# A fused attention and gated-MLP block: strided q, k, v weights, a new opening and one ring of weight tiles

## The chip, the cores and the metric

The kernel runs on one core of a Trainium2 chip. The metric is the device time of one execution in microseconds; lower is better. A core has a matrix engine (TensorE, PE in the rows; its weight loads are shown apart as PEld), VectorE (DVE), ScalarE (ACT), GpSimd (POOL) and SyncE (SP, which here only issues DMA transfers). The engines run at the same time, each through its own list of instructions in order, and wait for each other by semaphores. Matrices come from DRAM into on-chip memory (SBUF, 128 partitions); TensorE writes its results into PSUM, from where VectorE or ScalarE takes them out.

## The reference

One sequence of 2048 rows and 1024 columns, all in bf16:

```python
xn = layernorm(x)                                  # x: 2048 x 1024
q, k, v = split(xn @ wqkv)                         # 32 heads of 32 columns each
# a row attends to itself and to rows s-2, s-4, ... s-14 (W = 8, dilation 2), rows below 0 masked
attn = softmax(mask(q . k[s - 2w]) * 32 ** -0.5)   # over the 8 offsets w
s = (sum over w of attn * v[s - 2w]) @ wo
g = silu((silu(xn @ w1) * (xn @ w3)) @ w2)         # inner width 3584
out = x + s * g
```

## The kernel before

The rows are worked in four chunks (c) of 512. Within a chunk everything is held transposed: xnT has the 1024 columns of xn on partitions, as 8 tiles (kt) of 128, and 512 rows of the chunk along the free side. A group is eight matmuls that add up over kt into one PSUM tile of 128 x 512, each with its own weight tile of 128 x 128 as the stationary side.

TensorE's work in a chunk, in order: 24 groups for q, k, v (qkv, L291; 192 matmuls); 14 gate/up blocks (up_block, L261; four groups each, 448 matmuls) that give 28 tiles h; the first half of the down projection (down_half, L449; 112 matmuls); of the second half three steps of 16 matmuls; the output projection of attention (wo_proj, L420; 64 matmuls); and the other four steps. In the last chunk the output projection comes before the second half (last_half, L487). Chunk 0 is opened by hand (L503 to L668): layernorm of four row tiles, their transposes on TensorE, then two gate/up blocks (LEAD), of which the first one's groups are computed in halves of 256 rows (part0, L591), then its q, k, v groups, then the other 12 blocks.

Attention is done by VectorE beside TensorE. The columns of q, k, v are dealt so that a partition holds one head and one of four quarters (r) of its columns, and 8 columns (j) lie along the free side. Products of q with shifted k are summed over j into E; 16 GpSimd transfers (shuffle_out, L341) bring E into the layout L4 with heads and row quarters on partitions; softmax is done there; 16 more transfers (shuffle_back, L382) bring the weights pb back into Pr; products with shifted v are joined into oT, which the output projection reads.

The dealing needs every eighth weight column in one stationary tile. Before, the q, k, v weights were loaded as they are (raw), copied by VectorE and ScalarE into the dealt order (permute, L516; 24 copies of 128 x 1024) in chunk 0, used from there (pm), and written to a DRAM scratch wperm, from which chunks 1 to 3 load tiles of 256 columns. The heads' order on partitions is r, then head.

Order: the program's order is fixed by hand. Work for VectorE, ScalarE and GpSimd that lies beside TensorE is put into a list (Side, L17) with an estimated cost; after each group, side.step adds the group's time (GRP, 1.727) to a clock and a credit, and takes items off the list while there is credit and an item's due time has come. side.flush takes out what is left; wo_proj begins with it.

Queues: SP issues the weight tiles (512 KB each) in the order of use, each as soon as its buffer is free. There are two rings: wstream with 6 tiles for q, k, v, w1, w3 (load_w, L150) and w2s with 3 for w2 (load_w2, L175). In the last three gate/up blocks of a chunk load_w is not called (AHEAD); late_w calls it in the down projection. The weights of the output projection (load_wo, L189; 8 transfers of 256 KB) are issued after block 10, the residual rows xres after step 4 of the first down half. GpSimd issues the shuffles and most of the output.

Of the kernel before, what the change touches and what calls it, by code (L numbers as in the profile page):

```python
# [45 lines left out]
def kernel(  # L46
# [11 lines left out]
    nc = tc.nc  # L58
# [11 lines left out]
    NR = 4  # L70
    GRP = 1.727
    LEAD = 2
    WO_AT = 3
    AHEAD = 3
# [7 lines left out]
    wo_r = A_wo.rearrange("(h r j) n -> r h j n", r=NR, j=NJ)  # L82
# [3 lines left out]
    dram = ctx.enter_context(tc.tile_pool(name="dram", bufs=1, space=bass.MemoryType.DRAM))  # L86
# [5 lines left out]
    wstream = ctx.enter_context(tc.tile_pool(name="wstream", bufs=6))  # L92
    w2s = ctx.enter_context(tc.tile_pool(name="w2s", bufs=3))
# [9 lines left out]
    wperm = dram.tile([KT, P, 3 * NJ, P], BF16, name="wperm")  # L103
# [4 lines left out]

    x0 = [xp.tile([P, D], BF16, tag="x", name=f"x0_{st}") for st in range(NST)]
    for st in range(NST):  # L110
        nc.sync.dma_start(out=x0[st][:], in_=x_flat[st * P:(st + 1) * P, :])
    eps_t = const.tile([P, 1], FP32, name="eps_t")
# [23 lines left out]

    w_list = []
    for fb in range(LEAD):
        w_list += [("1", fb), ("3", fb)]
    for fb in range(LEAD, FB):  # L140
        w_list += [("1", fb), ("3", fb)]
    for c in range(1, NCH):
        w_list += [("q", b) for b in range(12)]
        for fb in range(FB):
            w_list += [("1", fb), ("3", fb)]
    w_list += [("2", fb) for fb in range(4)]
    w_next = iter(w_list)
    w_tiles = deque()

    def load_w():  # L150
        item = next(w_next, None)
        if item is None:
            return
        kind, i = item
        wt = wstream.tile([P, KT, 2 * P], BF16, tag="w")
        if kind == "q":
            src, dst = wperm[:, :, 2 * i:2 * i + 2, :].rearrange("kt kp tj p -> kp kt (tj p)"), wt[:]
        elif kind == "2":
            src = w2_r[:, i * 4:(i + 1) * 4, 512:1024]
            dst = wt[:].rearrange("p a b -> p (a b)").rearrange("p (i n) -> p i n", n=512)  # L160
        else:
            src, dst = (w1_r if kind == "1" else w3_r)[:, :, i * 256:(i + 1) * 256], wt[:]
        nc.sync.dma_start(out=dst, in_=src)
        w_tiles.append((item, wt if kind != "2" else dst))

    def take_w(item):
        got, wt = w_tiles.popleft()
        assert got == item, (got, item)
        return wt

    w2_list = [(c, dh, fb) for c in range(NCH) for dh in range(2) for fb in range(7) if (c, dh) != (NCH - 1, 1) or fb >= 4]
    w2_next = iter(w2_list)
    w2_tiles = deque()

    def load_w2():  # L175
        item = next(w2_next, None)
        if item is None:
            return
        c, dh, fb = item
        wt = w2s.tile([P, 4, 512], BF16, tag="w2")  # L180
        nc.sync.dma_start(out=wt[:], in_=w2_r[:, fb * 4:(fb + 1) * 4, dh * 512:(dh + 1) * 512])
        w2_tiles.append((item, wt))

    def take_w2(item):
        got, wt = w2_tiles.popleft()
        assert got == item, (got, item)
        return wt

    def load_wo():  # L189
        was = []  # L190
        for dh in range(2):
            wa = block("wo").rearrange("p (j n) -> p j n", n=CH)
            for r in range(NR):
                nc.sync.dma_start(out=wa[r * 32:(r + 1) * 32, :, :], in_=wo_r[r, :, :, dh * 512:(dh + 1) * 512])
            was.append(wa)
        return was
# [11 lines left out]

# [38 lines left out]

    brings = deque()

    def bring_one():  # L250
        if brings and brings[0][0] <= side.now:
            brings.popleft()[1]()

# [7 lines left out]
    def up_block(c, xnT, fb):  # L261
        hts = []
        w1t, w3t = take_w(("1", fb)), take_w(("3", fb))
        for i in range(2):
            pss = []
            for wt in (w1t, w3t):
                ps = psum_mm.tile([P, CH], FP32, tag="mm", name=f"gu{c}_{fb}_{len(pss)}")
                for kt in range(KT):
                    nc.tensor.matmul(  # L269
                        ps[:], lhsT=wt[:, kt, i * P:(i + 1) * P], rhs=xnT[:, kt, :],  # L270
                        start=(kt == 0), stop=(kt == KT - 1),
                    )
                pss.append(ps)
            if i == 1 and fb < FB - AHEAD:
                load_w()
                load_w()
# [5 lines left out]

    def proj_group(ps, lhs, xnT):
        for kt in range(KT):
            nc.tensor.matmul(ps[:], lhsT=lhs(kt), rhs=xnT[:, kt, :], start=(kt == 0), stop=(kt == KT - 1))  # L285

# [4 lines left out]
    def qkv(c, xnT):  # L291
        nc.gpsimd.tensor_copy(out=kT[:, :, 0:HALO], in_=kT[:, :, CH:CH + HALO])
        nc.gpsimd.tensor_copy(out=vT[:, :, 0:HALO], in_=vT[:, :, CH:CH + HALO])
        for b in range(12):
            wt = take_w(("q", b))
            for i in range(2):
                t, j = divmod(2 * b + i, NJ)
                ps = psum_mm.tile([P, CH], FP32, tag="mm", name="ps_qkv")
                proj_group(ps, lambda kt: wt[:, kt, i * P:(i + 1) * P], xnT)
                if i == 1:  # L300
                    load_w()
# [442 lines left out]
```

## Time and profile before

| what | value |
|---|---|
| median of 3 runs | 825.02 us (822.5 to 826.67) |
| profiled execution, span | 824.7 us |
| TensorE busy | 813.0 us, 99% |
| VectorE, ScalarE, GpSimd busy | 479.7, 206.8, 92.3 us |
| DMA, mean | 185 GB/s, 152.69 MB |

No time is given for the profiled execution beside its span; the span lies inside the three times. Times in the rows are microseconds from the span's start, and a row of a group gives busy time and mean ns of one instruction. In a row of the timeline stand start, length, engine, line, operation, output<-input, partitions x elements and, in brackets, how long the engine had been idle and what released it. A matmul's length in the rows includes its way through the pipeline, so the pace is read from the starts of neighbouring runs.

### The profile page before, as it was taken

What the parts mean: (1) busy time and instruction counts of PE and PEld (TensorE: products, weight loads), DVE (VectorE), ACT (ScalarE), POOL (GpSimd) and SP (SyncE); (2) the same over time, 40 slices, a digit from 0 to 9 for tenths busy, and PEclk for the clock granted to TensorE, in tenths of its full rate; (3) what the DMA queues carried; (4) which work ended last, traced back from release to release, by engine and by line L of the source; (5) the groups of instructions that cost most, each with busy time, mean ns of one, the idle gap of its engine ahead of it and who ended that gap; (6) DMA issues with size and microseconds to landing.
All of it is one profiled execution on the core that took longest, in us unless ns stands there. A gap on an engine that the chain in (4) does not pass through costs nothing.

```text
span 824.7 us, 9542 instructions
## 1 busy us (share of the span) xinstructions
PE 813.0 (99%) x3823; PEld 373.1 (45%) x3823; DVE 479.7 (58%) x486; ACT 206.8 (25%) x319; POOL 92.3 (11%) x172
## 2 busy tenths in 40 slices
PE   8999999998999999999999999999999999999998
PEld 5444444443444444444444444444444444444444
DVE  5739775594209947494222977569312595649432
ACT  6742132012232133101233213310113321311120
POOL 0000213101100041200110021300011004030010
PEclk9999999999999999999999999999999999999999
DMA  9992889692455698939355489995925557684820
GB/s 296 354 344 60 223 195 207 164 314 88 154 153 146 193 211 193 238 106 312 107 179 153 132 223 195 209 186 159 300 81 179 151 152 185 176 205 98 260 98 26
DMA packets 221821, 152.69 MB, mean 185 GB/s; under 512 B 19536, under 2 KB 208592, under 8 KB 221776
## 3 DMA queue, kind: packets, MB, share of 16 engines
q1 hardware_dynamic: 216336, 140.00, 62.3%
q0 software_dynamic: 5440, 12.07, 6.4%
q8 instruction: 30, 0.49, 0.3%
q14 instruction: 15, 0.12, 0.1%
HBM read 130.02 MB, written 10.49 MB: 170 GB/s over the span
## 4 chain that ended last, share of the span: by engine, by line
PE 90%; DVE 4%; DMA 3%; issue 1%; ACT 1%; POOL 0%; SPq 0%; DVEq 0%; ACTq 0%
PE gu L269 38%; PE ps_qkv L285 20%; PE acc L459 20%; PE ps_wo L428 7%; PE acc L495 3%; DMA Pr<-pb 2%; PE gu L285 1%; DVE pv L397 1%; DMA wt<-wperm 1%; DVE ht L258 1%; PE gu L594 1%; DVE stats L200 1%; DMA x<-in_A_x_dram 0%; POOL Pr L386 0%; ACT L256 0%
## 5 line engine op out<-in xcount | busy, mean ns | idle before, releaser
L269 PE MATMUL gu<-xnT_next,wt 128*128 128x512 bf16 x1344 | 290.6, 379 | 0.0
L269 PEld LDWEIGHTS <-wt 128*128 128x128 bf16 x1728 | 169.1, 98 | 203.9
L459 PE MATMUL acc<-wt,ht 128*128 128x512 bf16 x784 | 170.5, 379 | 0.8 <-DVE ht L258 0.8
L258 DVE TENSOR_TENSOR ht<-sg,gu 128x512 bf16<-128x512 bf16 x112 | 75.8, 680 | 95.6 <-PE gu L269 70.5
L256 ACT ACTIVATE sg<-gu 128x512 bf16<-128x512 f32 x112 | 65.9, 597 | 255.8 <-PE gu L269 230.3
L285 PE MATMUL ps_qkv<-xnT_next,wt 128*128 128x512 bf16 x576 | 124.8, 379 | 0.0
L315 DVE TENSOR_TENSOR prod<-qT,kT 128x4096 bf16<-128x4096 bf16 x32 | 73.1, 2285 | 85.8 <-ACT kT L289 85.8
L459 PEld LDWEIGHTS <-ht 128*128 128x128 bf16 x784 | 76.7, 98 | 93.5 <-issue 1.1
L285 PEld LDWEIGHTS <-wt 128*128 128x128 bf16 x608 | 59.5, 98 | 71.5
L445 DVE TENSOR_TENSOR gt<-gt,s_sb 128x512 f32<-128x512 f32 (+1 forms) x33 | 22.2, 673 | 119.4 <-ACT gt L439 73.0
L269 PE MATMUL gu<-xnT,wt 128*128 128x512 bf16 x384 | 83.0, 379 | 0.0
L345 POOL DMA_DIRECT2D L<-E x64 | 37.1, 587 | 292.5 <-DVE E L330 191.2
L397 DVE TENSOR_TENSOR pv<-Pr,vT 128x4096 bf16<-128x4096 bf16 x28 | 63.2, 2284 | 0.0
L326 DVE TENSOR_TENSOR prod<-prod 128x2048 bf16<-128x2048 bf16 x64 | 61.1, 955 | 1.4
L428 PE MATMUL ps_wo<-wo,oT 128*128 128x512 bf16 x256 | 57.6, 387 | 3.5 <-DMA wt<-wperm 3.5
L439 ACT ACTIVATE gt<-acc 128x512 f32<-128x512 f32 (+1 forms) x33 | 19.3, 584 | 147.6 <-PE acc L459 126.1
L386 POOL DMA_DIRECT2D Pr<-pb x64 | 36.8, 583 | 110.9 <-DVE pb L379 100.5
L447 POOL DMA_DIRECT2D out_dram<-o_t x28 | 15.3, 547 | 296.2 <-DVE o_t L446 295.0
L285 PE MATMUL ps_qkv<-xnT,pm 128*128 128x512 bf16 x192 | 41.9, 379 | 1.1 <-DVE pm L519 1.1
L428 PEld LDWEIGHTS <-oT 128*128 128x128 bf16 x256 | 25.4, 100 | 35.2 <-DVE oT L408 4.0
L432 ACT CAST s_sb<-ps_wo 128x512 bf16<-128x512 f32 x32 | 18.7, 585 | 72.9 <-PE ps_wo L428 72.9
L408 DVE TENSOR_TENSOR oT<-oT,pv 128x4096 bf16<-128x4096 bf16 x16 | 36.6, 2288 | 0.3
(69 smaller groups left out, 364.2 us busy)
## 6 DMA issues: line engine op xcount, KB each, us to landing
wt<-in_B_w_dram SPq DMA_DIRECT2D x168, 512.0 KB, 4.7
wt<-wperm SPq DMA_DIRECT2D x36, 512.0 KB, 4.9
wo<-in_A_wo_dram SPq DMA_DIRECT2D x32, 256.0 KB, 9.4
raw<-in_A_wqkv_dram SPq DMA_DIRECT2D x6, 1024.0 KB, 9.8
wperm<-pm SPq DMA_DIRECT2D x6, 1024.0 KB, 11.6
L<-E POOLq DMA_DIRECT2D x64, 64.0 KB, 5.9
Pr<-pb POOLq DMA_DIRECT2D x64, 64.0 KB, 5.6
xres<-in_A_x_dram SPq DMA_DIRECT2D x4, 1024.0 KB, 7.3
```

Of the source, the lines that this page charges most:

```text
L256: nc.scalar.activation(out=sg[:], in_=g_ps[:], func=ACTF.Silu)
L258: nc.vector.tensor_mul(ht[:], sg[:], u_ps[:])
L269: nc.tensor.matmul(ps[:], lhsT=wt[:, kt, i * P:(i + 1) * P], rhs=xnT[:, kt, :], start=(kt == 0), stop=(kt == KT - 1),)
L285: nc.tensor.matmul(ps[:], lhsT=lhs(kt), rhs=xnT[:, kt, :], start=(kt == 0), stop=(kt == KT - 1))
L315: nc.vector.tensor_mul(prod, qT[:], kT[:, :, o:o + CH])
L326: nc.vector.tensor_add(prod[:, 0:n, :], prod[:, 0:n, :], prod[:, n:2 * n, :])
L345: nc.gpsimd.dma_start(out=L4[sq * 32:(sq + 1) * 32, r, :, :], in_=E[r * 32:(r + 1) * 32, :, sq * P:(sq + 1) * P],)
L386: nc.gpsimd.dma_start(out=Pr[r * 32:(r + 1) * 32, :, sq * P:(sq + 1) * P], in_=pb[sq * 32:(sq + 1) * 32, :, :],)
L397: nc.vector.tensor_mul(dst, Pr[:, w, :].unsqueeze(1).to_broadcast([P, NJ, CH]), vT[:, :, o:o + CH])
L408: nc.vector.tensor_add(a, a, b)
L428: nc.tensor.matmul(ps[:], lhsT=oT[:, j, st * P:(st + 1) * P], rhs=was[dh][:, j, :], start=(j == 0), stop=(j == NJ - 1),)
L459: nc.tensor.matmul(accs[st][:], lhsT=hts[f][:, st * P:(st + 1) * P], rhs=w2t[:, i, :], start=(f == 0), stop=(f == FT - 1),)
```

## The change

- The scratch wperm, the raw loads and the permuting copies are gone. The q, k, v weights are loaded as they are, four tiles of two kt by 1024 columns for each of q, k and v, in every chunk. A group takes its stationary tile out of them as every eighth column: the access pattern has a step of 8 elements (16 bytes) where it had 1.
- The order of heads on partitions becomes head, then r, so both shuffles read or write partitions with a step of 4 on one side, and the weights of the output projection are loaded with two transfers of 1 MB in place of eight.
- Chunk 0: no gate/up block comes first. Layernorm of the four row tiles is reordered (row tile 0 loaded in two halves; tile 2 takes ScalarE's statistics), transposes go into the other PSUM pool, and six q groups are opened together: all six take kt 0 to 7 in turn for the first 256 rows, then each is finished for the second 256 rows; two more q groups follow at full width. Then k and v, then all 14 gate/up blocks.
- All weight tiles share one ring of nine buffers in the order of use; load_w is called in every block and step. The q, k, v buffers come free four at a time.
- The residual rows are loaded after step 1 of the down projection.
- In the last chunk the output projection leaves out its last tile (row tile 3, second column half). It is computed after the last down group, in pieces of 384 and 128 columns, and VectorE multiplies it straight from PSUM. The last down group is no longer cut in two.

The diff, cut to its core:

```diff
-    LEAD = 2
-    AHEAD = 3
+    NS = 9
-    wo_r = A_wo.rearrange("(h r j) n -> r h j n", r=NR, j=NJ)
+    wo_r = A_wo.rearrange("(p j) n -> p j n", j=NJ)
-    wstream = ctx.enter_context(tc.tile_pool(name="wstream", bufs=6))
-    w2s = ctx.enter_context(tc.tile_pool(name="w2s", bufs=3))
+    wstream = ctx.enter_context(tc.tile_pool(name="wstream", bufs=NS))
...
+    for c in range(NCH):
+        w_list += [("q", t, a) for t in range(3) for a in range(4)]
+        for fb in range(FB):
+            w_list += [("1", fb), ("3", fb)]
+        w_list += [("2", dh, fb) for dh in range(2) for fb in range(7)]
...
+            if item[0] == "q":
+                _, t, a = item
+                view = wt.rearrange("p (k c) -> p k c", k=2)
+                src = wqkv_r[:, 2 * a:2 * a + 2, t * D:(t + 1) * D]
...
+    def take_q(t):
+        tiles = [take_w(("q", t, a)).rearrange("p k (c j) -> p k j c", j=NJ) for a in range(4)]
+        return lambda kt, j: tiles[kt // 2][:, kt % 2, j, :]
...
+    for h in range(2):
+        nc.sync.dma_start(out=x0[0][:, h * 512:(h + 1) * 512], in_=x_flat[0:P, h * 512:(h + 1) * 512])
+    for st in range(1, NST):
         nc.sync.dma_start(out=x0[st][:], in_=x_flat[st * P:(st + 1) * P, :])
+    load_w(4, cuts=2)
+    load_w(NS - 4)
...
-            if i == 1 and fb < FB - AHEAD:
-                load_w()
-                load_w()
+            if i == 1:
+                load_w(2)
...
+    def qkv(c, xnT, ts):
+        for t in ts:
+            w = take_q(t)
...
+            for j in range(NJ):
                 ps = psum_mm.tile([P, CH], FP32, tag="mm", name="ps_qkv")
+                mm_group(ps[:], lambda kt: w(kt, j), lambda kt: xnT[:, kt, :])
+                if j == NJ - 1:
+                    load_w(4)
                 proj_out(t, j, ps)
                 side.step(GRP)
+            if t == 1:
                 qk_side(c)
...
+        E_r = E.rearrange("(h r) w s -> r h w s", r=NR)
-                    out=L4[sq * 32:(sq + 1) * 32, r, :, :], in_=E[r * 32:(r + 1) * 32, :, sq * P:(sq + 1) * P],
+                    out=L4[sq * NH:(sq + 1) * NH, r, :, :], in_=E_r[r, :, :, sq * P:(sq + 1) * P],
...
+        for n0, w in ((0, 384), (384, 128)):
+            ps = wo_piece(att["oT"], was, NST - 1, CH + n0, w)
+            finish(c, NST - 1, CH + n0, w, gt[:, n0:n0 + w], ps[:, 0:w], xres, nc.sync)
...
-    busy(warm, 12)
+    busy(warm, 14)
...
+    wq = take_q(0)
+    qps = [psum_mm.tile([P, CH], FP32, tag="mm", name="ps_qkv") for _ in range(NOPEN)]
+
+    def part(kt, js, h):
+        cs = slice(h * 256, (h + 1) * 256)
+        for j in js:
+            nc.tensor.matmul(
+                qps[j][:, cs], lhsT=wq(kt, j), rhs=xnT[:, kt, cs],
+                start=(kt == 0 and h == 0), stop=(kt == KT - 1), skip_group_check=True,
+            )
...
+    for kt in range(4):
+        part(kt, OPEN, 0)
+    tp3 = pe_transpose(3)
+    copy_in(tp3, 3, LO, V)
+    copy_in(tp3, 3, HI, A)
+    part(4, OPEN, 0)
+    part(5, OPEN, 0)
+    tp2 = pe_transpose(2)
...
+    for kt in (6, 7):
+        part(kt, OPEN, 0)
+    for j in OPEN:
         for kt in range(KT):
+            part(kt, (j,), 1)
+        proj_out(0, j, qps[j])
+    for j in range(NOPEN, NJ):
+        ps = psum_mm.tile([P, CH], FP32, tag="mm", name="ps_qkv")
+        mm_group(ps[:], lambda kt: wq(kt, j), lambda kt: xnT[:, kt, :])
+        proj_out(0, j, ps)
+    load_w(4)
...
-    w1t, w3t = take_w(("1", 1)), take_w(("3", 1))
...
-            proj_group(ps, lambda kt: pmh[t, kt // 4][:, kt % 4, j, :], xnT)
-            proj_out(t, j, ps)
-            permute_some(2)
...
     for c in range(NCH):
+        qkv(c, xnT, (1, 2) if c == 0 else (0, 1, 2))
...
-            if fb == 4:
+            if fb == 1:
                 res["x"] = load_xres(c)
...
-            s_sb = wo_proj(c, was)
+            s_sb = wo_proj(every[:-1], was)
```

360 lines of the change are left out of this document (116 added, 244 removed).

## The prediction

> **What bounds the kernel now.** I read the page's busy times first, then the list of TensorE runs in order of time with their idle times, then who TensorE waited for, then the stages around each wait. The page and the table of stages (window, length, busy us with counts of PE, PEld, DVE, ACT and POOL, granted clock, DMA share, GB/s):
>
> ```profile
> span 824.7 us, 9542 instructions
> PE 813.0 (99%) x3823; PEld 373.1 (45%) x3823; DVE 479.7 (58%) x486; ACT 206.8 (25%) x319; POOL 92.3 (11%) x172
> ...
> 0.00:9.90 9.90, 7.86 (x35) 3.12 (x36) 5.13 (x14) 6.27 (x13) 1.46 (x10) 1.00 0.81 234
> 189.24:192.66 3.42, 3.42 (x11) 1.36 (x12) 0.26 (x1) 0.58 (x1) 0.00 (x0) 0.67 0.12 42
> 820.63:824.70 4.07, 0.00 (x1) 0.00 (x0) 0.85 (x2) 0.38 (x1) 0.00 (x0) 1.00 0.06 16
> ```
>
> TensorE is the bound almost everywhere, so what counts is what its time holds beside useful matmuls. Its runs (start, length, count; idle in brackets):
>
> ```profile
> 9.90 1.05 PE L594 MATMUL gu<-xnT,wt 128*128 128x256 bf16 x8
> 14.93 3.65 PE L594 MATMUL gu<-xnT,wt 128*128 128x256 bf16 x32 [0.23 <-ACT xnT L556]
> 18.42 7.07 PE L285 MATMUL gu<-xnT,wt 128*128 128x512 bf16 x32
> 25.33 1.46 PE L285 MATMUL ps_qkv<-xnT,pm 128*128 128x512 bf16 x6
> 68.17 83.04 PE L269 MATMUL gu<-xnT,wt 128*128 128x512 bf16 x384
> 151.05 34.70 PE L459 MATMUL acc<-wt,ht 128*128 128x512 bf16 x160
> 189.24 15.67 PE L428 MATMUL ps_wo<-wo,oT 128*128 128x512 bf16 x64 [3.50 <-DMA wt<-wperm]
> 204.75 13.98 PE L459 MATMUL acc<-wt,ht 128*128 128x512 bf16 x64
> 218.56 41.60 PE L285 MATMUL ps_qkv<-xnT_next,wt 128*128 128x512 bf16 x192
> 260.00 96.86 PE L269 MATMUL gu<-xnT_next,wt 128*128 128x512 bf16 x448
> 418.86 41.60 PE L285 MATMUL ps_qkv<-xnT_next,wt 128*128 128x512 bf16 x192
> 556.99 2.75 PE L459 MATMUL acc<-wt,ht 128*128 128x512 bf16 x12
> 620.11 41.60 PE L285 MATMUL ps_qkv<-xnT_next,wt 128*128 128x512 bf16 x192
> ```
>
> From 218.56 to 260.00 stand 192 matmuls: 215.8 ns each. A chunk has 928, the kernel 3712: 801.2 us. The remaining 23.5 us, start to start:
> - 9.90 until the first useful matmul;
> - 9.90 to 18.42 for 64 half-width matmuls worth 6.91: 1.61 lost (transposes, copies);
> - 25.33 to 68.17 for 192 worth 41.44: 1.40 lost, waiting for permuted weights;
> - 151.05 to 189.24 for 160 worth 34.53: 3.66 lost ahead of chunk 0's output projection;
> - 189.24 to 204.75 for 64 worth 13.81: 1.70 lost, at a granted clock of 0.67 in its first 3.4 us;
> - chunk 1 (218.56 to 418.86) nothing; chunk 2 (201.25 for 200.30) 0.95; chunk 3 0.2; the tail 4.07.
>
> The profile puts chunk 0's wait down to a load of q weights, which this projection doesn't read; what ended last before 189.24 is VectorE's final join of attention (186.89 + 2.29). Chunk 1's same join ended 11 us before the end of its own first down half (356.7 + 34.5):
>
> ```profile
> 133.00 1.22 DVE L379 TENSOR_TENSOR pb<-z,mx 128x1024 bf16<-128x1024 f32 x1
> 154.72 2.29 DVE L397 TENSOR_TENSOR oT<-Pr,vT 128x4096 bf16<-128x4096 bf16 x1 [6.17 <-DMA Pr<-pb]
> 186.89 2.29 DVE L408 TENSOR_TENSOR oT<-oT,pv 128x4096 bf16<-128x4096 bf16 x1
> 343.07 2.29 DVE L397 TENSOR_TENSOR oT<-Pr,vT 128x4096 bf16<-128x4096 bf16 x1 [6.13 <-DMA Pr<-pb]
> 358.68 2.28 DVE L408 TENSOR_TENSOR oT<-oT,pv 128x4096 bf16<-128x4096 bf16 x1
> 377.85 2.29 DVE L408 TENSOR_TENSOR oT<-oT,pv 128x4096 bf16<-128x4096 bf16 x1
> 544.79 2.29 DVE L397 TENSOR_TENSOR oT<-Pr,vT 128x4096 bf16<-128x4096 bf16 x1 [7.57 <-DMA Pr<-pb]
> 559.81 0.68 DVE L258 TENSOR_TENSOR ht<-sg,gu 128x512 bf16<-128x512 bf16 x1
> ```
>
> **The change, part by part. Chunk 0's order.** All of q, k, v now precedes the gate/up blocks, so VectorE's attention work starts two blocks earlier: in its order the first product with Pr comes after h tile 23 instead of 27, four h tiles, 4 x 16 x 215.8 ns = 13.8 us. Before, pb ended 16.8 us ahead of the end of the up blocks (134.2 against 151.05); now 30.6. The shuffle to Pr took 20.5 us from there in chunk 0, 17.3 in chunk 1 by the rows (325.75 to 343.07), so the first product starts 10 to 13 us ahead of the down projection, and its chain, 34.5 us before (154.72 to 189.18), plus four more h tiles of 0.6, ends 24 to 27 us into work of 34.5. The 3.66 goes, and with no idle time ahead of it the 1.70 of low clock too: -5.36. The cover left is 8 us; next behind it would be the s_sb copies, which follow each projection group.
>
> **No permutation.** 16 VectorE and 8 ScalarE copies, six 1 MB raw loads, six 1 MB writes of wperm and their waits go: TensorE's 1.40 to 0. Their engine time was otherwise beside matmuls.
>
> **The strided weights.** Of the 768 q, k, v weight loads in 512-wide steps 720 remain full width; 96 half-width matmuls open six groups. Each load now takes every eighth column, which no row of this trace does on TensorE. The nearest rows: eight plain loads in a row, and copies of 1024 elements read with a stride against unstrided passes of the same size:
>
> ```profile
> 7.15 0.45 PEld L552 LDWEIGHTS <-x 128*128 128x128 bf16 x8 [1.53 <-DVE x L203]
> L519 ACT COPY pm<-raw 128x1024 bf16<-128x1024 bf16 x8 | 15.6, 1949 | 0.0
> L561 ACT ACTIVATE junk<-x 128x1024 bf16<-128x1024 bf16 x1 | 1.1, 1057 | 1.9 <-DMA x<-in_A_x_dram 1.9
> L519 DVE COPY pm<-raw 128x1024 bf16<-128x1024 bf16 x16 | 15.9, 1090 | 2.2 <-DMA raw<-in_A_wqkv_dram 2.2
> L203 DVE TENSOR_SCALAR x<-x,mv,rs 128x1024 bf16<-128x1024 bf16 x4 | 2.2, 546 | 0.1
> ```
>
> Loads can follow each other every 56 ns (0.45 / 8). A stride costs ScalarE 1.84 times, VectorE 2.0. Low end: nothing, since the load lies under a 215.8 ns matmul; a gain is excluded, because unstrided loads are hidden already. High end: each column at ScalarE's strided 1.90 ns, 128 x 1.90 = 243 ns: 720 x 27 + 96 x 134 = 32.3 us. I take twice 56, 113 ns: hidden under full width, and 4 ns over the half-width pace of 109 (14.93 to 18.42 / 32), 0.4 us; TensorE is nearer to a doubling, as both engines that show one agree. The Trainium skill, "SBUF — State Buffer", section "Door 1: The DMA port swizzle", says that reads need two hits per 16-byte line and pay for each new line; here every column is its own line. By it alone the sum would be anywhere between those ends; by "TensorE: Matmul & The Clock Gate", section "Weight-path perf modes", fast loading takes "4 chunks of 32 columns, packed or strided", and the cost would be 0.
>
> **The start.** Loads of x stay first on SP's queue; tile 0 comes in halves. The rows that price the chain:
>
> ```profile
> 5.76 0.69 DVE L200 BATCH_NORM_STATS2 st<-x 128x6 f32<-128x512 bf16 x1 [0.82 <-DMA x<-in_A_x_dram]
> 6.55 0.55 DVE L203 TENSOR_SCALAR x<-x,mv,rs 128x1024 bf16<-128x1024 bf16 x1
> 7.16 0.62 PE L552 MATMUL tp<-ident,x 128*128 128x128 bf16 x8 [0.79 <-DVE x L203]
> ```
>
> The root of tile 0 no longer queues behind ScalarE's pass over another tile, which puts its normalization near 5.6, but 14 warm-up matmuls hold TensorE to 6.7 and its transpose ends at 7.3. Then ScalarE copy 0.6, root 0.3, VectorE reciprocal and normalization 0.7, transpose 0.6, copy 0.4, with hand-overs: first useful matmul about 10.1 (+0.2). From there 96 half-width at 109 and 16 full, 13.9 us, two transposes of 0.45 and 0.4 of strided loads: 15.2 for 13.8 worth, 1.4 lost against 1.61. So the start stands at 0.0; from -1.0 (TensorE follows the chain at once) to +1.0 (tile 1 lands as late as the third tile did here, 5.76). The q weights: x is 1 MB and q 2 MB; at the 234 GB/s of the first row of stages 2.3 MB are there by 9.9, the last by about 12.5, needed at 14.9. Kept cover: 2 us.
>
> **One ring of nine** instead of six and three; same 512 KB per 3.45 us of matmul, q tiles freed four at a time with five ahead (a 13.8 us cover for 2 MB). SP's queue is moved past nothing that blocks: the residual load, now three steps earlier, takes a buffer that chunk 1's second join frees (360.96), and is issued two steps into the down projection, at 363.6. Cost 0. **Shuffles** read partitions with a stride of four: same bytes and counts, 0, bounds in the second rival. **The tail.** Silu goes off the end, but the 384-wide piece's two VectorE passes queue ahead of the 128-wide ones:
>
> ```profile
> 820.67 0.38 ACT L439 ACTIVATE gt<-acc 128x256 f32<-128x256 f32 x1 [2.67 <-PE acc L495]
> 821.08 0.42 DVE L445 TENSOR_TENSOR gt<-gt,s_sb 128x256 f32<-128x256 f32 x1 [2.17 <-ACT gt L439]
> 803.10 0.69 DVE L445 TENSOR_TENSOR gt<-gt,s_sb 128x512 f32<-128x512 f32 x1 [11.31 <-ACT gt L439]
> ```
>
> Between 0.42 at 256 and 0.69 at 512 lie 0.56 at 384 and 0.29 at 128: 2 x 0.56 + 2 x 0.29 less the 0.45 of the last eight matmuls is 1.25, against 0.38 + 2 x 0.42 = 1.22 now. 0, between -0.6 (nothing queues: 0.58) and +0.3 (two more hand-overs).
>
> **Sum:** -5.36 - 1.40 + 0.0 = -6.8 on a span of 824.7: 817.9. The three times before have a median of 825.0, 0.3 above this span, so 818.2.
>
> **Rivals.** *First, strided loads outlast a matmul* (ends slower). For it: ScalarE's 1.90 ns per strided column; against: the 56 ns of a plain load, a quarter of the cover. It decides from about 180 ns, where the half-width steps alone eat the gain (96 x 71 = 6.8); past 216 each further ns costs 0.8 us. Time at 243 ns: 850. The "SBUF — State Buffer" rule above is this rival's. *Second, Pr lands later.* Before, SP issued no weight tile between the first and the last of these rows, while the projection's weights and Pr shared the DMA:
>
> ```profile
> 334.44 2.10 SPq L163 DMA_DIRECT2D wt<-in_B_w_dram  x2
> 337.04 0.58 POOL L386 DMA_DIRECT2D Pr<-pb  x1 [0.62 <-DMA Pr<-pb]
> 360.34 7.28 SPq L181 DMA_DIRECT2D wt<-in_B_w_dram  x3
> ```
>
> Now loads go on through the last three blocks. Chunk 2's 0.95 is exactly this: Pr 1.4 us later than chunk 1's in its chunk, the h tile that frees a PSUM buffer ending at 560.49. So chunk 1 has 0.5 us to spare and chunk 2 none: 2 us more give +3.5 (821.7), 5 us about +16 with chunks 0 and 3 (834). Against: Pr's last transfer was issued by 337.6, and the added loads come from about 341 (one block of 6.9 after 334.4). Break-even near 3 us. *Third, chunk 0's wait stays*, if Pr is late there by 10 us: 823.5.
>
> **How the numbers follow.** Forecast 0.64 (its own range 814 to 821), first rival 0.16, second 0.13 (half of it still faster, a third about the same), third 0.07. 0.5%, 4.1 us, is about what a measurement tells from no change. Faster 0.73, same 0.09, slower 0.18. The range 813 to 826 leaves out the first rival and the worst of the second.
>
> **What would show it.** TensorE's idle ahead of chunk 0's projection gone and the clock at 1.00 there; no wait of q matmuls; 192 q, k, v matmuls still in 41.4 us (longer: first rival, and the mean of those weight loads says by how much); acc waiting on ht in chunks 1 and 2 by no more than 1 us (longer: second); first q matmul near 10, the first k matmul near 25. Wrong if q, k, v take over 45 us a chunk.

## The result and the profile after

The changed kernel takes 819.62 us (median of 7 runs, 818.27 to 820.12) beside 825.02 for the kernel before (7 runs on the same chip, 822.5 to 827.23): a ratio of 0.9943, with a 95% interval of 0.9925 to 0.9962. It is faster by 5.4 us, 0.57%; the interval reaches from 0.4% to 0.75%, around the 0.5% that the prediction takes as about what a measurement tells from no change. The prediction was 818.2, in a range of 813 to 826.

The page of the profiled execution opens so:

```profile
span 816.5 us, 9525 instructions
PE 809.6 (99%) x3820; PEld 406.2 (50%) x3820; DVE 464.8 (57%) x472; ACT 191.5 (23%) x310; POOL 92.4 (11%) x172
```

Weight loads (PEld) hold 33 us more than before and the span is 8.2 us shorter: the loads became longer beside the matmuls, not between them. TensorE's runs in order of time (start, length, line, operation, count; idle in brackets), with one stretch out of chunk 0's output projection (window, length, busy us with counts of PE, PEld, DVE, ACT and POOL, granted clock, DMA share, GB/s):

```profile
9.72 2.78 PE L563 MATMUL ps_qkv<-xnT,wq 128*128 128x256 bf16 x24 [0.52 <-DVE xnT L521]
12.34 0.61 PE L517 MATMUL tp<-ident,x 128*128 128x128 bf16 x8
...
21.11 31.24 PE L245 MATMUL ps_qkv<-xnT,wq 128*128 128x512 bf16 x144
52.19 96.86 PE L245 MATMUL gu<-xnT,w 128*128 128x512 bf16 x448
148.88 34.70 PE L454 MATMUL acc<-w,ht 128*128 128x512 bf16 x160
183.42 13.98 PE L409 MATMUL ps_wo<-wo,oT 128*128 128x512 bf16 x64
187.30:190.80 3.50, 3.50 (x18) 1.61 (x17) 2.82 (x5) 1.22 (x3) 1.14 (x2) 1.00 0.19 68
197.23 13.98 PE L454 MATMUL acc<-w,ht 128*128 128x512 bf16 x64
211.04 41.60 PE L245 MATMUL ps_qkv<-xnT_next,wq 128*128 128x512 bf16 x192
252.48 96.86 PE L245 MATMUL gu<-xnT_next,w 128*128 128x512 bf16 x448
...
411.34 41.60 PE L245 MATMUL ps_qkv<-xnT_next,wq 128*128 128x512 bf16 x192
...
549.47 34.99 PE L454 MATMUL acc<-w,ht 128*128 128x512 bf16 x160
...
611.93 41.60 PE L245 MATMUL ps_qkv<-xnT_next,wq 128*128 128x512 bf16 x192
...
810.49 1.91 PE L409 MATMUL ps_wo<-wo,oT 128*128 128x384 bf16 x16
```

After the 0.52 us ahead of the first q matmul at 9.72, TensorE waits nowhere in chunk 0, and the granted clock in the output projection is 1.00. Start to start, the same account as in the prediction, in us lost beside useful matmuls at 215.8 ns:

| stage | before | after | difference |
|---|---|---|---|
| until the first useful matmul | 9.90 | 9.72 | -0.18 |
| half-width opening (after: 9.72 to 21.11 for 10.36 of work) | 1.61 | 1.03 | -0.58 |
| q, k, v behind permuted weights | 1.40 | 0 | -1.40 |
| idle ahead of chunk 0's output projection | 3.66 | 0 | -3.66 |
| low clock in that projection (after: 183.42 to 197.23 = 13.81) | 1.70 | 0 | -1.70 |
| chunk 1, chunk 2, chunk 3 with the tail | 5.24 | 4.57 | -0.67 |

The differences make the 8.2 us between the two spans. Each run's time is its span and some 1.75 us (1.7 to 1.9 over all runs): 818.27 belongs to 816.5, 820.12 to 818.3. Before's profiled span of 824.7 therefore belongs to an execution of about 826.5, above its median, and after's profiled one is 1.35 below its own. That is why 8.2 us between the profiles are 5.4 between the medians.

VectorE's attention in the changed kernel: pb of chunk 0, its first product with Pr, its last join, and chunk 2's first product:

```profile
117.03 1.23 DVE L364 TENSOR_TENSOR pb<-z,mx 128x1024 bf16<-128x1024 f32 x1
136.11 2.29 DVE L383 TENSOR_TENSOR oT<-Pr,vT 128x4096 bf16<-128x4096 bf16 x1 [3.53 <-DMA Pr<-pb]
170.42 2.29 DVE L394 TENSOR_TENSOR oT<-oT,pv 128x4096 bf16<-128x4096 bf16 x1
536.62 2.29 DVE L383 TENSOR_TENSOR oT<-Pr,vT 128x4096 bf16<-128x4096 bf16 x1 [6.91 <-DMA Pr<-pb]
```

The join ends at 172.71, 10.7 us ahead of the projection that reads it (183.42); before, it ended 0.06 ahead of it, with TensorE waiting. The shuffle from pb's start to the first product takes 19.1 us; before, it took 21.7 (133.00 to 154.72). Below, "the shuffle" is always this time, from the start of pb to the first product with Pr.

### The profile page after: what moved, and what is told of

Its sections match the earlier page's. It is cut to its first block, busy times and chain, and to the rows that moved or that the text cites. A ratio compares the mean times of both kernels' runs of the same rounds, so it can differ in the third digit from the quotient of the medians.

```text
span 816.5 us, 9525 instructions
## 1 busy us (share of the span) xinstructions
PE 809.6 (99%) x3820; PEld 406.2 (50%) x3820; DVE 464.8 (57%) x472; ACT 191.5 (23%) x310; POOL 92.4 (11%) x172
## 4 chain that ended last, share of the span: by engine, by line
PE 91%; DVE 4%; DMA 2%; issue 1%; ACT 1%; POOL 0%; SPq 0%; DVEq 0%; ACTq 0%
PE gu L245 40%; PE acc L454 20%; PE ps_qkv L245 19%; PE ps_wo L409 7%; PE acc L477 3%; DMA Pr<-pb 2%; PE ps_qkv L563 1%; DVE pv L383 1%; DVE ht L251 1%; DVE stats L190 1%; POOL Pr L372 0%; DMA x<-in_A_x_dram 0%; ACT L249 0%; DVE oT L394 0%; DVE pv L394 0%
## 5 line engine op out<-in xcount | busy, mean ns | idle before, releaser
L245 PE MATMUL gu<-xnT_next,w 128*128 128x512 bf16 x1344 | 290.6, 379 | 0.0
L245 PEld LDWEIGHTS <-w 128*128 128x128 bf16 x1792 | 175.3, 98 | 211.2
L454 PE MATMUL acc<-w,ht 128*128 128x512 bf16 x784 | 170.5, 379 | 0.1
L245 PEld LDWEIGHTS <-wq 128*128 128x128 bf16 x720 | 103.3, 143 | 52.1
L245 PE MATMUL ps_qkv<-xnT_next,wq 128*128 128x512 bf16 x576 | 124.8, 379 | 0.0
L245 PE MATMUL gu<-xnT,w 128*128 128x512 bf16 x448 | 96.9, 379 | 0.0
L434 DVE TENSOR_TENSOR gt<-gt,s_sb 128x512 f32<-128x512 f32 x31 | 21.4, 690 | 125.2 <-ACT gt L428 67.7
L409 PE MATMUL ps_wo<-wo,oT 128*128 128x512 bf16 (+2 forms) x264 | 56.1, 373 | 0.0
L428 ACT ACTIVATE gt<-acc 128x512 f32<-128x512 f32 x32 | 19.1, 597 | 148.8 <-PE acc L454 127.0
L245 PE MATMUL ps_qkv<-xnT,wq 128*128 128x512 bf16 x144 | 31.2, 379 | 0.0
```

Of the source, the lines that this page charges most:

```text
L245: nc.tensor.matmul(ps, lhsT=lhs(kt), rhs=rhs(kt), start=(kt == 0), stop=(kt == KT - 1))
L409: nc.tensor.matmul(ps[:, 0:w], lhsT=oT[:, j, st * P:(st + 1) * P], rhs=was[dh][:, j, n0:n0 + w], start=(j == 0), stop=(j == NJ - 1),)
L454: nc.tensor.matmul(accs[st][:], lhsT=hts[f][:, st * P:(st + 1) * P], rhs=w2t[:, i, :], start=(f == 0), stop=(f == FT - 1),)
```

## The experiments

Two questions were open after the result: whether strided weights cost anything, hidden or not, and whether chunk 0's wait went because of the order of the work, as the prediction had it, or because Pr arrives faster.

**Neighbouring columns.** The q, k, v groups read 128 neighbouring columns, so q, k and v come out in another order of channels than the projection's weights.

```diff
-        tiles = [take_w(("q", t, a)).rearrange("p k (c j) -> p k j c", j=NJ) for a in range(4)]
+        tiles = [take_w(("q", t, a)).rearrange("p k (j c) -> p k j c", j=NJ) for a in range(4)]
```

> The changed kernel with one edit: a q, k, v group reads 128 neighbouring weight columns in place of every eighth one (the heads are then dealt wrongly, so the output is not the reference's; the work is the same). Theory: the strided load (143 ns in the rows against 98 plain) lies under the 215.8 ns matmul and under the 109 ns half-width one, so nothing changes: q, k, v take 41.4 us a chunk in both, the 96 half-width matmuls about 109 ns each, and the time is that of the changed kernel within 0.5 us, the loads back at 98 ns. Rival: the longer loads cost TensorE something that its modelled rows do not show; then this kernel is faster than the changed one by more than 1 us.

Measured: 819.49 us (818.59 to 820.24), a ratio of 0.9957 [0.9942, 0.9971] to before: the changed kernel's time. Weight loads of q, k, v by line and form (busy us, mean ns of one, idle), first of the changed kernel:

```profile
L245 PEld LDWEIGHTS <-wq 128*128 128x128 bf16 x720 | 103.3, 143 | 52.1
```

and of this one:

```profile
L245 PEld LDWEIGHTS <-wq 128*128 128x128 bf16 x720 | 70.4, 98 | 84.7
```

A strided load's record is 45 ns longer, and it costs nothing under a 512-wide matmul, nor under a 256-wide one: the opening's first 24 matmuls come every (12.34 - 9.72) / 24 = 109 ns, the pace of the kernel before, and with neighbouring columns every (12.71 - 10.09) / 24 = 109 ns too. So the stride costs this kernel nothing that can be seen.

**Where the stride would show.** q, k, v groups in four 128-row passes, with a weight load ahead of each 128-wide matmul; strided, and with neighbouring columns.

```diff
-                mm_group(ps[:], lambda kt: w(kt, j), lambda kt: xnT[:, kt, :])
+                for cs in (slice(i * P, (i + 1) * P) for i in range(NST)):
+                    mm_group(ps[:, cs], lambda kt: w(kt, j), lambda kt: xnT[:, kt, cs])
```

> The changed kernel with all q, k, v groups but chunk 0's first eight done in four passes of 128 rows (2816 matmuls 128 wide in place of 704 at 512), stationary columns strided. It prices the strided load by itself, with no wide matmul to hide it. Theory: the load takes about 100 ns (56 ns of a plain one, plus the 45 ns by which its row is longer), and at most 109, the half-width pace seen: 24 groups then take 768 x 100 = 77 us a chunk in place of 41.4, the whole 120 to 155 us more. Rival: the load is as quick as a plain one and only its row is longer: 56 ns a matmul, 43 us a chunk, about 6 us more in all.

> As the run with strided columns in passes of 128 rows, but with 128 neighbouring columns (dealt wrongly, so not the reference's output). Both theories: 56 ns a matmul, 43 us for 24 groups, about 6 us more than the changed kernel. The difference of the two runs, over 2816, is the price of the stride.

Measured: 841.82 strided and 825.07 plain, one run each. Chunk 1's q, k, v groups on TensorE, up to the first gate/up matmul, strided:

```profile
215.86 47.71 PE L245 MATMUL ps_qkv<-xnT_next,wq 128*128 128x128 bf16 x768
263.41 96.86 PE L245 MATMUL gu<-xnT_next,w 128*128 128x512 bf16 x439
```

and plain:

```profile
212.32 43.04 PE L245 MATMUL ps_qkv<-xnT_next,wq 128*128 128x128 bf16 x768
255.20 96.86 PE L245 MATMUL gu<-xnT_next,w 128*128 128x512 bf16 x439
```

Start to start a load and its matmul take 47.55 / 768 = 61.9 ns strided and 42.88 / 768 = 55.8 plain. The two times agree: (841.82 - 825.07) / 2816 is 5.9 ns. So a strided load holds TensorE for no more than 61.9 ns, and the expectation of some 100, taken from the 143 ns of the record, was wrong: a record's length is not how long the load keeps TensorE busy.

What a plain load takes by itself these two runs don't show. The plain pace goes with the width of the matmul: 215.8 ns at 512 rows, 109.2 at 256, 55.8 at 128. From 512 to 256 it falls by 106.6, and from 256 to 128 by 53.4, half as much for half as many rows. So at 128 the matmul still sets the pace and the plain load is still hidden. The stride costs at least 6.1 ns a load where no wider matmul covers it; whether it also doubles the load, as it about doubles a pass of ScalarE or VectorE, stays open.

**The order undone.** Two gate/up blocks of chunk 0 go back ahead of k and v, everything else as changed:

```diff
+    LEAD = 2
-        w_list += [("q", t, a) for t in range(3) for a in range(4)]
-        for fb in range(FB):
+        lead = LEAD if c == 0 else 0
+        w_list += [("q", 0, a) for a in range(4)]
+        for fb in range(lead):
+            w_list += [("1", fb), ("3", fb)]
+        w_list += [("q", t, a) for t in (1, 2) for a in range(4)]
+        for fb in range(lead, FB):
...
-        qkv(c, xnT, (1, 2) if c == 0 else (0, 1, 2))
-        for fb in range(FB):
+        lead = LEAD if c == 0 else 0
+        for fb in range(lead):
+            hts += up_block(c, xnT, fb)
+        qkv(c, xnT, (1, 2) if c == 0 else (0, 1, 2))
+        for fb in range(lead, FB):
```

> The changed kernel with chunk 0's first two gate/up blocks put ahead of its k and v groups, as far ahead as they stood before the change; everything else stays. Theory: the order alone removed the wait ahead of chunk 0's output projection. Attention then starts 13.8 us later, its last join moves from 172.7 to about 186.5 or a little later, the projection is due at 183.4: 3 to 5 us of idle and about 1.7 us of low clock come back, 5 to 7 us in all (span 821.5 to 823.5). Rival: the wait went because the permuting copies and the transfers of wperm no longer stood in the way; then under 1 us of idle ahead of the projection, and no change of time.

Measured: 820.66 us (819.54 to 826.17, 7 runs), a ratio of 0.9973 [0.9943, 1.0003] to before. In its profile, chunk 0's pb and first product with Pr, and TensorE's projection:

```profile
131.29 1.22 DVE L369 TENSOR_TENSOR pb<-z,mx 128x1024 bf16<-128x1024 f32 x1
149.86 2.29 DVE L388 TENSOR_TENSOR oT<-Pr,vT 128x4096 bf16<-128x4096 bf16 x1 [3.04 <-DMA Pr<-pb]
184.39 13.99 PE L414 MATMUL ps_wo<-wo,oT 128*128 128x512 bf16 x63 [0.59 <-DVE oT L399]
```

The last join moved from 172.71 to 184.33, by 11.6 us where 13.8 was expected; but only 0.59 us of the wait came back, not 3.66, and no low clock. So the theory that the old order by itself makes the wait is too simple. With the old order the kernel stands on the edge: five of its runs stayed under 821.5, one took 822.69 at a mean granted clock of 0.998, and one 826.17 at 0.996. What else had gone is time in the shuffle, 18.6 us here against 21.7 before. That is the whole difference between the two profiles: pb starts 18.0 us ahead of the down projection in both, and from the first product to the last join it takes 34.5 us in both. Two changed transfers could have made it quicker: pb, E and Pr now on every fourth partition instead of 32 neighbouring ones, and the projection's weights, which travel at the same time, in two transfers of 128 partitions instead of eight of 32.

**Each old transfer with the old order.** Both are the kernel with LEAD = 2 and one edit more; the first brings back neighbouring partitions in the shuffles, the second the eight transfers:

```diff
-                    out=L4[sq * NH:(sq + 1) * NH, r, :, :], in_=E_r[r, :, :, sq * P:(sq + 1) * P],
+                    out=L4[sq * NH:(sq + 1) * NH, r, :, :], in_=E[r * 32:(r + 1) * 32, :, sq * P:(sq + 1) * P],
-                    out=Pr_r[r, :, :, sq * P:(sq + 1) * P], in_=pb[sq * NH:(sq + 1) * NH, :, :],
+                    out=Pr[r * 32:(r + 1) * 32, :, sq * P:(sq + 1) * P], in_=pb[sq * NH:(sq + 1) * NH, :, :],
```

```diff
-            nc.sync.dma_start(out=wa, in_=wo_r[:, :, dh * 512:(dh + 1) * 512])
+            for r in range(NR):
+                nc.sync.dma_start(out=wa[r * 32:(r + 1) * 32, :, :], in_=wo_r[r * 32:(r + 1) * 32, :, dh * 512:(dh + 1) * 512])
```

The first of them sums the products of other partitions into a head than the changed layout of q and k has there; the second computes the same as the changed kernel.

> The run with two gate/up blocks ahead of k and v, with both shuffles reading and writing 32 neighbouring partitions as before the change instead of every fourth (heads land on wrong partitions, so the output is not the reference's; bytes and counts are the same). In the run with two blocks ahead, Pr came 17.4 us after pb and TensorE waited 0.6 us; before the change it was 20.5 us and 3.7 us plus 1.7 of low clock. Theory A, the stride of four made the shuffle quicker: Pr about 20 us after pb, a wait of 3 us or more ahead of the projection, and about 3 us more time than with the stride. Theory B, the partitions do not matter: 17 to 18 us, a wait under 1 us, the same time.

> The run with two gate/up blocks ahead of k and v, with the projection's weights loaded in eight transfers of 256 KB on 32 partitions each, as before the change, instead of two of 1 MB on all. These loads are issued while Pr's shuffle is under way. Theory A (partitions of the shuffle): nothing changes, Pr 17 to 18 us after pb. Theory B, the eight transfers held Pr up: Pr about 20 us after pb, a wait of 3 us or more ahead of chunk 0's projection, and about 3 us more time.

Measured: 822.96 (820.87 to 826.18, 10 runs) and 824.51 (822.02 to 826.39, 10 runs), ratios of 0.9992 [0.9972, 1.0011] and 1.0004 [0.9987, 1.0022] to before. With the old shuffle, TensorE's projection and two stretches behind the wait:

```profile
187.37 16.84 PE L414 MATMUL ps_wo<-wo,oT 128*128 128x512 bf16 x64 [3.79 <-DVE oT L399]
187.30:190.80 3.50, 3.43 (x9) 1.24 (x10) 0.01 (x1) 0.00 (x0) 0.00 (x0) 0.50 0.00 0
190.80:194.20 3.40, 3.40 (x12) 1.34 (x11) 1.39 (x2) 0.91 (x2) 0.58 (x1) 0.65 0.00 0
```

and with the eight transfers:

```profile
186.07 15.67 PE L415 MATMUL ps_wo<-wo,oT 128*128 128x512 bf16 x64 [2.12 <-DVE oT L400]
```

Chunk 0's shuffle takes 22.0 and 20.4 us in them, the wait is 3.79 and 2.12, and the low clock costs 2.9 and 1.7. Neither kernel can be told from the kernel before: either old form, with the old order, brings back what it had, though the second wait is shorter than the 3 us expected. Neither has permuting copies or a scratch wperm, so the wait doesn't need those.

How much of the 18.6, 22.0 and 20.4 us belongs to the form of the transfers is less sure, since each is one profile, and the same shuffle differs between profiles. Up to chunk 0's projection, the changed kernel, the one with neighbouring columns and the one with a reworked start (further down) differ only in their opening or in which columns a weight load takes, and their chunk 0 shuffles take 19.1, 17.2 and 18.0 us. Chunk 1 is steadier: 17.2 to 17.3 us in the five profiles that have the changed transfers and the changed kernel's loads there, 18.0 with the old shuffle.

A low clock shows in some runs and not in others. Five runs of the kernel with the old shuffle, at a mean granted clock of 1.0, took 820.9 to 822.4; its other five, at 0.996 to 0.998, took 823.5 to 826.2. Of 25 runs of the kernel before on the same chip, 14 at 0.999 or 1.0 took 821.6 to 823.6, and 11 at 0.998 or less 824.3 to 827.3. The clock of 0.998 fits one stretch of 3.4 us at half clock somewhere in the run, which is 1.7 of 825 us. That those runs met it in this wait is likely from the profiles, but not shown, since one run of each kernel was profiled.

**The other corner: new order, both old transfers.** The changed kernel with both edits above.

> The changed kernel with both transfer forms of before: 32 neighbouring partitions in the shuffles (heads land on wrong partitions, so the output is not the reference's) and the projection's weights in eight transfers. Only the order of chunk 0 then stands against the wait. Theory: Pr comes about 22 us after pb starts in chunk 0, as before, but attention starts 13.8 us earlier, so the last join still ends 7 us ahead of the projection and TensorE does not wait there. In chunks 1 and 2 the first product with Pr comes about 1 us later, and what TensorE loses in chunk 2 grows from 0.3 to 1 to 1.7 us: about 1 to 2 us more than the changed kernel, 820.5 to 822. Rival: with the old forms the chunk 0 wait comes back in spite of the order (823 or more).

Measured: 820.63 (819.17 to 822.79, 10 runs), a ratio of 0.9945 [0.9927, 0.9964] to before. TensorE in chunk 0 and chunk 2:

```profile
183.57 13.97 PE L410 MATMUL ps_wo<-wo,oT 128*128 128x512 bf16 x64
554.05 32.10 PE L455 MATMUL acc<-w,ht 128*128 128x512 bf16 x148 [0.91 <-DVE ht L252]
```

Nothing waits ahead of the projection: the new order takes the wait away with both old transfers too. Chunk 2 loses 1.81 us in this profile where the changed kernel's lost 0.29, about as expected; but it lost 1.45 in the profile with neighbouring columns, whose transfers are the changed ones, so most of that difference can come from one execution to the next. The corners together; the runs were made on several chips, so the ratio to the kernel before on the same chip is what can be compared:

| chunk 0's order | transfers | us | ratio to before | wait in the profile, us |
|---|---|---|---|---|
| new | new | 819.62 | 0.9943 [0.9925, 0.9962] | 0 |
| new | both old | 820.63 | 0.9945 [0.9927, 0.9964] | 0 |
| old | new | 820.66 | 0.9973 [0.9943, 1.0003] | 0.59 |
| old | shuffle old | 822.96 | 0.9992 [0.9972, 1.0011] | 3.79 |
| old | projection weights old | 824.51 | 1.0004 [0.9987, 1.0022] | 2.12 |

In the profiles either half of the change removes all or nearly all of the wait. In the times only the two kernels with the new order are clear of the kernel before; the old order with the new transfers lies between, and its interval touches 1. What is sure of the order is its margin: the join ends 10.7 us ahead of the projection, and 10.3 with both old transfers, where the old order leaves none.

**One block more.** LEAD = 3, the block beyond the edge:

> The changed kernel with three gate/up blocks of chunk 0 ahead of its k and v groups (two gave 0.6 us of wait). Theory: from there each block more delays the last join by its 6.9 us, less what VectorE gains: 6 to 7.5 us of idle ahead of the projection, and behind it about 1.7 us of low clock, 8 us more than with two. Rival: VectorE's list has slack and takes the delay up; under 3 us of idle.

Measured: 831.61 (830.63 to 832.0, 4 runs), 11 us more than with two blocks, where 8 was expected.

```profile
193.76 16.62 PE L414 MATMUL ps_wo<-wo,oT 128*128 128x512 bf16 x64 [10.06 <-DVE oT L399]
```

10.06 us of idle, more than the 6 to 7.5 expected, and 2.64 of low clock. Against two blocks, pb starts 6.6 us later, the block's own time, and the shuffle takes 21.8 us, 3.3 more. Its transfers have the changed form here, so a slow shuffle doesn't need the old one; what slowed this one was not tried.

**Only the moment of the load.** In the kernel before, the projection's weights are loaded at the last up block:

```diff
-            if fb == 10:
+            if fb == FB - 1:
```

> The kernel before, with one edit: the projection's weights (eight transfers of 256 KB) are loaded after the last gate/up block instead of after block 10, so that they no longer run beside Pr's shuffle. Theory: chunk 0's wait came from two things together, the late start of attention and a shuffle slowed by these loads and by its own 32 neighbouring partitions. With the loads out of its way Pr comes 17 to 19 us after pb starts instead of 21.7, the wait of 3.5 us shrinks to about 1 us or goes, the low clock behind it with it, and the times, which ranged from 821.6 to 827.3, lie near 820 to 822. Rival: the loads are no hindrance; Pr at 21 us or more, the same times.

Measured: 824.38 (10 runs) beside 825.18, a ratio of 0.9997 [0.9978, 1.0016]: no gain, where 820 to 822 was expected. In its profile chunk 0 did improve:

```profile
186.99 13.99 PE L428 MATMUL ps_wo<-wo,oT 128*128 128x512 bf16 x64 [1.74 <-DVE oT L408]
```

1.74 us of idle where 3.50 stood before, and no low clock, with a shuffle of 20.0 us; but the shuffles of chunks 1 and 2 came 0.7 and 0.5 us later, chunk 2 lost 1.48 instead of 0.95, and the median stayed. Nine of the ten runs have a mean clock of 0.999 or 1.0, yet they range from 822.8 to 825.5, so the clock is not all of the spread; the rest has no cause shown here. Moving the load in time is not what the change gained by.

**Seven weight buffers** instead of nine.

```diff
-    NS = 9
+    NS = 7
```

> The changed kernel with seven buffers in the ring instead of nine, the fewest with which it works. Theory: four are held by the group's q, k or v tiles, three are ahead, so the last of the next four is asked for only when its first group runs, and lands 4 to 5 us later than it is issued (3.8 us median for such a tile): 2 to 4 us of wait at the two changes inside q, k, v of each chunk, 15 to 30 us in all. Rival: loads are quick enough, under 3 us in all; then nine buffers are not what keeps TensorE fed.

Measured: 829.95, one run. TensorE's waits for q weights (us in total, times, longest):

```profile
PE ps_qkv L245 <- DMA wq<-in_A_wqkv_dram: 10.3, 8, 1.5
```

This is less than the 15 to 30 expected, but the cover of nine buffers is real: with two fewer, TensorE waits 1.2 to 1.5 us six matmuls into k and six into v, in every chunk. There each group's seventh weight tile comes from the last of the four loads, the one that the expectation had late.

**Two places left, the start and the tail.** 11 and 4 warm-up matmuls for 14 and 6, tile 1's root and tile 0's copies ahead of ScalarE's sum over tile 2, tile 1's transpose ahead of tile 3's statistics, and halves at the end:

```diff
-        for n0, w in ((0, 384), (384, 128)):
+        for n0, w in ((0, 256), (256, 256)):
...
-    busy(warm, 14)
+    busy(warm, 11)
...
-    nc.scalar.activation(out=junk[:], in_=x0[2][:], func=ACTF.Identity, accum_out=tot[:])
-    nc.scalar.mul(out=nm[:], in_=tot[:], mul=-1.0 / (32.0 * D))
...
-    busy(x0[0], 6)
-    copy_in(tp0, 0, HI, A)
+    busy(x0[0], 4)
...
+    copy_in(tp0, 0, HI, A)
...
+    nc.scalar.activation(out=junk[:], in_=x0[2][:], func=ACTF.Identity, accum_out=tot[:])
+    nc.scalar.mul(out=nm[:], in_=tot[:], mul=-1.0 / (32.0 * D))
```

> The changed kernel with its opening and tail reworked: ScalarE makes tile 1's root before its sum over tile 2, VectorE takes tile 1 before tile 3's statistics, 11 and 4 warm-up matmuls for 14 and 6; the last two pieces are 256 and 256 columns for 384 and 128. Theory: the first useful matmul comes at about 8.9 instead of 9.7 (-0.8), and VectorE's last pass ends 0.85 us after TensorE instead of 1.25 (-0.4): 1 to 1.2 us less. Rival for the start: fewer warm-up matmuls leave the clock low for longer and the half-width matmuls begin slow, so that up to 1 us is lost; rival for the tail: the two passes are hidden anyway, 0.

Measured: 818.17 (817.93 to 818.42, 6 runs), 0.9928 [0.9902, 0.9954] of before and 1.45 below the median of the change alone, which ran on another chip. The first useful matmul comes at 9.20 where 8.9 was expected (9.72 in the changed kernel's profile), and VectorE's last pass ends 0.4 us earlier against TensorE's end, as expected: 0.9 us together.

**The same with the projection's weights loaded at the last up block** (the edit of the load above):

> The run with the reworked opening and tail, with the projection's weights loaded after the last gate/up block instead of after block 10. Theory: Pr comes 1 us or more earlier in every chunk, chunk 2's 0.8 us ahead of its down projection goes, and the time falls by 0.5 to 1 us from 818.2. Rival: 2 MB at the head of the down projection hold up the w2 tiles in the same ring, and TensorE waits for weights there: slower.

Measured: 817.95 (817.40 to 818.41, 6 runs), 0.9914 [0.9891, 0.9937] of before. It is faster than the kernel before, and can't be told from the 818.17. In its profile Pr comes earlier in chunk 2 alone, by 0.4 us, and what chunk 2 loses falls from 0.82 to 0.37.

## Why the prediction was right, step by step

**The time.** 817.9 was the sum as a span, and the profiled span is 816.5, the runs' median span 817.8. As a time it was 1.4 low: the prediction set the span of 824.7 beside the median of 825.0 as if they were one quantity. Every run has some 1.75 us around its span, and that profiled execution was about 1.4 us slower than the median of its kernel. With 1.75 in place of the 0.3 the same sum gives 819.65, next to the 819.62 measured; but that is chance, since the gain was 8.2 in the profiled executions and 5.4 in the medians where 6.8 was worked out.

**Chunk 0's order, -5.36.** All of it went in the profiled execution, with the first product 12.8 us ahead of the down projection (predicted 10 to 13), the join 23.8 into its 34.5 (24 to 27) and a cover of 10.7 (8). The mechanism holds: with both old transfers the new order takes the wait away. It is half of the account. The prediction took the shuffle's 20.5 us as given and the order as the only cause; in its profile the old order with the quicker shuffle has 0.59 us of wait left. And -5.36 is the price in an execution that met the low clock; by their mean clock, more than half of the 25 runs of the kernel before that stand beside the old transfers didn't.

**No permutation, -1.40.** 52.19 - 21.11 is 31.08 for 144 matmuls worth 31.08: nothing left.

**Strided weights, 0.4.** 0 here: the half-width pace is 109 ns with strided and with neighbouring columns. The estimate of 113 ns a load was nearly twice the 61.9 in which a strided load and its matmul come, and the high end of 243, the first rival's ground, four times. The failed step is the 56 ns that were doubled: the row they come from is eight transposes, and 55.8 ns is the pace of a 128-wide matmul, under which a plain load is hidden. It is a bound on the load and not its length. That TensorE doubles as ScalarE and VectorE do was never put to the test by these runs. The forecast stood because 62 lies under 109 and both 62 and 113 lie under 215.8. The Trainium skill, "SBUF — State Buffer", section "Door 1: The DMA port swizzle", has each new 16-byte line cost something; the runs agree in sign, with 6 ns or more for 128 columns each in a line of its own. The Trainium skill, "TensorE: Matmul & The Clock Gate", section "Weight-path perf modes", counts strided columns with packed ones; the runs have 61.9 against 55.8 ns, and as the plain load's own time isn't shown, they don't decide how far that holds.

**The start, 0.0.** -0.76 in the profiled execution: 9.72 where 10.1 was predicted, 1.03 lost where 1.4 was. Inside the range given, and not all from the change: the 14 warm-up matmuls took 4.5 us here, and 5.6 to 5.7 in the profiles of the kernels with neighbouring columns and with two blocks ahead, which start alike; there the first useful matmul came at 10.1, as predicted. The warm-up matmuls reach their full pace sooner in one execution than in another, at a granted clock of 1.00 in the rows of both; why isn't shown.

**The ring, 0.** No q, k, v matmul waits for its weights; TensorE's waits beyond the warm-up are two, both at the start:

```profile
PE tp L517 <- DVE x L193: 0.9, 1, 0.9
PE ps_qkv L563 <- DVE xnT L521: 0.5, 1, 0.5
```

**The shuffles, 0, and the second rival.** In the two profiles they are 2.6 us quicker in chunk 0 and 0.7 to 1.3 in the others (18.5 to 17.2, 20.0 to 19.3, 16.6 to 15.7), where the prediction had them as before and the rival had them late. Chunk 1's gain is seen again in other profiles; in chunk 2 the changed transfers took 19.3 to 20.5 us over five profiles, around the 20.0 of before. The rival's price was right. Over eleven kernels, chunk 2's loss follows the start of its first product with Pr, counted from the chunk's start: 125.28 gives 0.29 (after), 125.93 gives 0.95 (before), 126.29 gives 1.31 (old order and shuffle), 126.80 gives 1.81 (new order, old transfers), each within 0.02 of the start less 124.99. The changed kernel's profile gained 0.66 there; with neighbouring columns, 126.44 gives 1.45.

**The tail, 0.** 4.28 us after TensorE's ideal end against 4.29. The four passes are as interpolated, 0.56 twice and 0.29 twice, and do queue:

```profile
812.06 0.55 DVE L434 TENSOR_TENSOR gt<-gt,ps_wo 128x384 f32<-128x384 f32 x1 [5.37 <-PE ps_wo L409]
812.65 0.56 DVE L435 TENSOR_TENSOR o_t<-gt,xres 128x384 bf16<-128x384 f32 x1
813.13 0.28 DVE L434 TENSOR_TENSOR gt<-gt,ps_wo 128x128 f32<-128x128 f32 x1
813.44 0.29 DVE L435 TENSOR_TENSOR o_t<-gt,xres 128x128 bf16<-128x128 f32 x1
```

**The third rival** needed Pr to be 10 us late in chunk 0, and it was earlier.

## What to carry to other kernels

When a wait stands at an edge, ask for every term of the chain that ends late, not only for the one that the change names: here the order was enough, the two transfer forms together nearly were, and only undoing one at a time showed that. A single profiled execution of such a kernel shows one side of a spread; weigh the gain read from it against the runs' median, span with span. A pace read from a row in which something else sets the pace is a bound and not a price: narrow the cover until the pace changes, and then price the difference.

## What the runs showed of the hardware

- A weight load of 128 columns 16 bytes apart and its 128-wide matmul take 61.9 ns start to start, neighbouring columns 55.8, which is the matmul's own pace; the load's record is 143 to 147 ns against 98. Under 256 rows or more the stride can't be seen.
- The drop in clock around an idle gap ahead of 64 matmuls, one profile for each gap: gaps of 0.59 and 1.74 us had none; gaps of 2.12, 3.50, 3.79 and 10.06 us cost 1.7, 1.7, 2.9 and 2.6 us. Read in steps of 1 us, the granted clock is 0.50 for 3.4, 3.4, 6.8 and 10.2 us, one, two or three times 3.4. Each cost is half of the part of that time which falls on matmuls, so it doesn't grow with the gap. After the two shorter of these gaps the clock stays at 1.00 for another 1.0 and 1.2 us of matmuls before it falls. The Trainium skill, "TensorE: Matmul & The Clock Gate", section "Part 1: The HAM clock gate", has half the clock after at least one idle window of about 3.4 us. The 0.50 agrees; the length doesn't, since a gap of 2.12 us was enough here.
- The same 16 transfers from pb to Pr, in the kernel with the old order and while the projection's weights were travelling, took 22.0 us on 32 neighbouring partitions and 18.6 on every fourth; with the new order and both old forms they took 19.5, and on every fourth partition with three blocks ahead 21.8. These are single profiles, of a time that differs by up to 1.9 us between profiles of kernels alike in it. What else sets it wasn't tried, and stays open.
